# Turning a 512x512 block on VectorE and in the transfers instead of on TensorE, and one stage of products prepared further ahead

## The chip, the cores and the metric

One core of one Trainium2 chip. The metric is the device time of one execution in microseconds; lower is better. Times inside a trace are microseconds from the start of the span.

## The reference

A token mixer gated by a channel MLP, in fp32, for 2048 tokens of 512 numbers:

```python
xn = layernorm(x)                                   # S = 2048, D = 512
s = attention(xn, wqkv) @ wo                        # 32 heads of 16, causal window of 256
y = layernorm(xn)
g = silu(gelu(y @ w1 + b1) @ w2 + b2)               # w1: 512 x 1792, w2: 1792 x 512
out = x + s * g
```

## The kernel before, in words

The attention runs first (to about 432 us of the trace); its output lies in DRAM as `oT_d`, its row sums as `rden_d`. Then the MLP runs over four chunks of 512 tokens. All large products are made of three fp32r products: an operand is split into a high part (an ACT copy to fp32r) and a low part (a VectorE subtraction), and high x high, high x low and low x high are summed.

The loop `for c in range(2)` (lines 1060 to 1155) does chunks 0 and 1. With `c == 1` each iteration `i` of 15 does, in this order:
- `activate(i)`: ACT makes `gelu` of bank `h(i)` into a `t2` tile (five buffers) and its high part `gh(i)`, VectorE the low part `gl(i)`. `gh` and `gl` have two buffers each.
- `project(i - 1)`: twelve products of `gh`, `gl` with w2 into the banks `acc`.
- `hidden(i + 2)`: twelve products of w1 tile i + 2 with the transposed y into a bank of `ps_st` (two banks).
- pieces of other work: the attention output of this chunk is loaded (`load_o`, two transfers), multiplied and split (`split_o`); and y of chunks 2 and 3 is prepared.

That last work is what the change touches. Four tiles of 128 tokens x 512 are loaded (`load_y`, `yp`, four buffers) and normalised twice (`steps2`; statistics on VectorE, a power on GpSimd, the application on ACT): chunk 2 in iterations 0 to 2, chunk 3 in iterations 5 to 7. Then y must be transposed, so that the 512 features lie on partitions as four tiles `kt`. Here `transposed` (line 986) does this by four TensorE transposes per tile into a bank of `ps_yt`: `first_y` for chunk 2 in iterations 3 and 4, `second_y` for chunk 3 in iterations 8 and 10.

Chunks 2 and 3 are then done together: their w1 products are made from seven instead of eight block products, of sums and differences of y and w1 blocks. The inputs are called `11`, `21`, `t1`, `t3`, `t2`, `22` and `t4`; each has two tiles, and each tile a high and a low half in the area of `big` that a w1 tile of chunks 0 and 1 leaves free (`halves_of`): t1 = y3 - y2 of the first half of features, t3 = y3's second half - its first, t2 = y3's second half - t1, t4 = y2's second half - t2. y2 itself is kept meanwhile in `gated[:, 2:4]` and in `kept[1]`. The loop over `g` from line 1160 makes these products.

TensorE, VectorE, ACT and GpSimd issue in the order in which the program is written (`Ordered`, line 32). The queue of transfers, SyncE, does so where `nc.sync.on` is set; elsewhere, so in the whole MLP part, a planner orders it by when it expects each transfer to be ready.

Of the kernel before, what the change touches and what calls it, by code (L numbers as in the profile page):

```python
# [9 lines left out]
F32 = mybir.dt.float32  # L10
# [8 lines left out]
P = 128  # L19
NCH = S // 512  # L20
NKB = S // P
KT = D // P
NF = F // P
# [27 lines left out]
def mixer_kernel(ctx, tc, x, wqk, wv, wo, w1, b1, w2, b2, out):  # L51


    nc = SimpleNamespace(**{name: Ordered(tc, name) for name in ("tensor", "vector", "scalar", "gpsimd", "sync")})

    const = ctx.enter_context(tc.tile_pool(name="const", bufs=1))
    bigp = ctx.enter_context(tc.tile_pool(name="bigp", bufs=1))
    t2 = ctx.enter_context(tc.tile_pool(name="t2", bufs=5))
    small = ctx.enter_context(tc.tile_pool(name="small", bufs=3))
    dram = ctx.enter_context(tc.tile_pool(name="dram", bufs=1, space=bass.MemoryType.DRAM))  # L60
# [8 lines left out]
    def split(dst_hi, dst_lo, src, eng=None):  # L69

        (eng or nc.scalar.copy)(dst_hi, src)
        nc.vector.tensor_sub(dst_lo, src, dst_hi.bitcast(F32))
# [103 lines left out]
    def open_slot(i):  # L176
# [9 lines left out]
    w_d = {"w1": dram.tile([P, NF * 512], F32, name="w1_d"), "w2": dram.tile([P, NF * 512], F32, name="w2_d"),  # L186
           "wo": dram.tile([P, 4 * 512], F32, name="wo_d")}
    g_d = dram.tile([NF, P, 512], F32, name="g_d")
    mT_d = dram.tile([NQ, NCH, 32, P], F32, name="mT_d")


# [6 lines left out]
    ps_st = early.enter_context(tc.tile_pool(name="ps_st", bufs=2, space=PSUM))  # L198
# [24 lines left out]
    ident = const.tile([P, P], F32, name="ident")  # L223
# [360 lines left out]
    mlp = {}  # L584
# [54 lines left out]
    def y_steps(a, b):  # L639
        run(mlp["ln"][a:b])  # L640
# [241 lines left out]
    def load_y(c):  # L882
        if c > 1:
            return load_x(c, ((mlp["yp"], "y"),), "y")
        return [load(mlp["yp"], "y", xn_d[4 * c + i], f"y_{c}_{i}") for i in range(4)]

    def fetch_sums():
        den = t2.tile([P, 512], F32, tag="t2", name="den")
        for g in range(4):
            nc.sync.dma_start(den[32 * g: 32 * g + 32], oT_d[g, :, DH].rearrange("a (c t) -> a c t", c=NCH))  # L890
        return den

    def load_o(c, g):

        cols = slice(512 * c, 512 * (c + 1))
        raw = load(t2, "t2", oT_d[g, :, 0:DH, cols], f"or_{c}_{g}")
        rec = mlp["w2", g // 2][:, 512 * (14 + g % 2): 512 * (15 + g % 2)].bitcast(F32)
        nc.sync.dma_start(rec, bass.AP(tensor=rden_d.tensor, offset=rden_d.offset + 8 * g * S + 512 * c,
                                       ap=[[S, 8], [0, DH], [1, 512]]))
        return raw, rec  # L900
# [70 lines left out]
    def inputs(name, kt, part):  # L971

        return area(halves_of[name, kt])[:, 512 * part: 512 * part + 512]

    yh1 = mlp["yy"][0][0], mlp["yy"][0][1]
    kept = {}
# [6 lines left out]
        first = 256 * (j % (2 if j < 4 else 4))  # L983
        return at[:, first: first + 256 * n]

    def transposed(c, kt):
        ps = ps_yt.tile([P, 512], F32, tag="b", name=f"yt_{c}_{kt}")
        for i in range(4):
            nc.tensor.transpose(ps[:, P * i: P * (i + 1)], mlp["y"][i][:, P * kt: P * (kt + 1)], ident)
        return ps  # L990

    def put(name, kt, src):

        split(inputs(name, kt, 0), inputs(name, kt, 1), src)

    def first_y(kt):

        ps = transposed(2, kt)
        nc.scalar.copy(kept[kt // 2][:, kt % 2], ps)
        put("21" if kt > 1 else "11", kt % 2, ps)  # L1000

    def second_y(kt):

        t1, t4 = kept[0][:, kt], kept[1][:, kt]
        t3, t2_ = (t2.tile([P, 512], F32, tag="t2", name=f"yt{k}_{kt}") for k in (3, 2))
        ps = transposed(3, kt)
        nc.vector.tensor_sub(t1, ps, t1)
        nc.scalar.copy(t3, ps)
        ps = transposed(3, kt + 2)
        nc.vector.tensor_sub(t2_, ps, t1)  # L1010
        nc.vector.tensor_sub(t3, ps, t3)

        def more():
            put("22", kt, ps)
            nc.vector.tensor_sub(t4, t4, t2_)
            put("t1", kt, t1)
            put("t3", kt, t3)

        def most():
            put("t2", kt, t2_)  # L1020
            put("t4", kt, t4)
        return more, most

    raw_w = {}

    def fetch_pair(g):
        raw_w[g] = [load(mlp["yp"], "y", w_d["w1"][:, 512 * f: 512 * f + 512], f"wr_{g}_{f}") for f in (g, g + 7)]
# [32 lines left out]
    for c in range(2):  # L1060
        accs = open_accs(c)
        gs, os_, hs, wanted = {}, [], {}, []
        made = ready if c == 0 else {}

        def hidden(f):
            hs[f] = ps_st.tile([P, 512], F32, tag="b", name=f"h_{c}_{f}")
            for k in range(3 * KT):
                hidden_mm(hs[f], f, k)

        def activate(f):  # L1070
            if f in made and f in soon:
                gs[f] = made[f]
                return
            src = made[f] if f in made else hs.pop(f)
            g = src if f in made and f < 2 else t2.tile([P, 512], F32, tag="t2", name=f"g_{c}_{f}")
            nc.scalar.activation(g, src, AF.Gelu_apprx_tanh, bias=b1s[:, f: f + 1])
            gs[f] = split_g(c, f, g, nc.scalar.copy)

        order = [2, 3, 0, 1, 4, 5, *range(6, NF)] if c == 0 else [*range(NF)]
        if c:  # L1080
            hidden(0)
            hidden(1)
        o_from, o_late = (0, 0) if c else (8, 1)
        for i in range(NF + 1):
            if i < NF:
                activate(order[i])
            if c and i in (1, 2, 6, 7):
                y_steps(6, 10)
            if c and i in (9, 11):
                rest[0]()  # L1090
            if c and i in (9, 12):
                rest[1]()
            if c and i == 14:
                kept["w"] = bigp.tile([P, 768], F32R, tag="wb1", name="wsh")
                combine_w(0)
            if c == 0:
                for kind, f in late_w[LATE[i]: LATE[i + 1]]:
                    settle(kind, f, nc.scalar.copy, nc.vector)
            if i >= 1:
                project(accs, [(order[i - 1], gs.pop(order[i - 1]))], order[0], order[-1])  # L1100
            if i + 2 < NF and order[i + 2] not in made and order[i + 2] > 1:
                hidden(order[i + 2])
            if c == 0:
                if i == 2:
                    den = fetch_sums()
                if 4 <= i < 8:
                    nc.vector.reciprocal(den[:, P * (i - 4): P * (i - 3)], den[:, P * (i - 4): P * (i - 3)])
                    if i == 7:
                        nc.sync.dma_start(rden_d.rearrange("g a (c t) -> (g a c) t", c=NCH), den)
                if i == 4:  # L1110
                    mlp["y"] = load_y(1)
                if i == 6:
                    mlp["ln"] = layernorm(mlp["y"], "C1", False)
                for back, (a, b) in enumerate(((0, 2), (2, 4), (4, 5), (5, 6), (6, 8), (8, 10))):
                    if i == 6 + min(back, 5):
                        y_steps(a, b)
            else:
                steps2(i)
                if i == 3:
                    kept[0] = gated[:, 2:4]  # L1120
                    first_y(0)
                    first_y(1)
                if i == 4:
                    kept[1] = bigp.tile([P, 2, 512], F32, tag="wb1", name="y2_21")
                    first_y(2)
                    first_y(3)
                    mlp["y"] = load_y(3)
                if i in (8, 10):
                    rest = second_y(i // 10)
                if i == 12:  # L1130
                    fetch_pair(0)
            k = i - o_from
            if 0 <= k - 2 - o_late < 4:
                os_.append(split_o(c, k - 2 - o_late, wanted[k - 2 - o_late][0]))
            if 0 <= k - 1 - o_late < 4:
                nc.vector.tensor_mul(wanted[k - 1 - o_late][0], *wanted[k - 1 - o_late])
            if 0 <= k < 4:
                wanted.append(load_o(c, k))
            if c and i in (0, 1, 5, 6):
                y_steps(5, 6)  # L1140
        if c == 0:
            gated = bigp.tile([P, 4, 512], F32, tag="wa", name="gated")

        def between(i):
            if c == 0 and i in (0, 2):
                y_transpose(1, i)
                y_transpose(1, i + 1)
                if i == 2:
                    mlp["y"] = load_y(2)
            if c == 1 and i in (1, 2):  # L1150
                split_w(0, 2 * i - 2)
                split_w(0, 2 * i - 1)
        end_chunk(c, accs, os_, between)
        if c == 0:
            steps2(-1)
# [148 lines left out]
```

## Time and profile before

| | us |
|---|---|
| median of 3 runs | 750.93 (750.61 to 751.13) |
| the profiled execution | 750.88 |
| its span | 749.2 |
| loop `c == 1`, first `hidden` to the last `project` | 489.16 to 568.97 |

In the profile all recorded instructions of the kernel stand at line 43, the helper that issues them, so groups are told apart by engine and tile name: `h` are the banks of `hidden`, `acc` those of `project`, `yt` those of the transposes of y, `s` those of the output product, `xnT` is `big`, `or` and `w` are the two loads of `load_o`, `wr` the raw w1 tiles, `xo` the loads of x for the end of a chunk. A timeline row gives start, duration, engine, operation and operands and, in brackets, how long the engine was idle before it and what ended that. SPq is SyncE's queue: its durations are those of the issue, not of the transfer.

### The profile page before, as it was taken

The page shows a single profiled execution, that of the slowest core. Times are in us where ns is not written, and L with a number is a line of the kernel's source. Part 1 is how long each engine was busy: PE and PEld are TensorE (multiplying, and loading weights), DVE is VectorE, ACT ScalarE, POOL GpSimd, SP SyncE. Part 2 cuts the span into 40 slices and gives each one's busy share as a digit, 9 for nine tenths or more (in the row PEclk, how much of TensorE's full clock was granted, in tenths as well). Part 3 has the DMA queues.
Part 4 walks back from the last instruction along what each step waited for, and adds up shares of the span by engine and source line. Part 5 has one row for each costly group of instructions (what it writes and reads, how often), then busy time and mean ns, then how long its engine had stood idle before and what let it go on. Part 6 is the DMA issues. An engine that isn't in the chain of part 4 may idle for free.

```text
span 749.2 us, 18758 instructions
## 1 busy us (share of the span) xinstructions
PE 733.9 (98%) x7408; PEld 590.4 (79%) x7408; DVE 511.7 (68%) x781; ACT 441.1 (59%) x746; POOL 299.3 (40%) x644
## 2 busy tenths in 40 slices
PE   8999999999999999999999999999999999999997
PEld 7886777777778888777776788888888888888886
DVE  7886777877766778887872648763576765676743
ACT  7757767867667676778877745444463744442001
POOL 7413757767666555767877600120102000001102
PEclk9999999999999999999999999999999999999999
DMA  8633356766555535647724482542012232253611
GB/s 288 191 74 78 84 133 149 201 168 183 152 142 145 144 90 142 162 111 190 200 86 148 133 286 94 165 151 82 31 45 102 93 100 72 70 174 123 222 45 56
DMA packets 56951, 99.40 MB, mean 133 GB/s; under 512 B 11104, under 2 KB 11360, under 8 KB 56864
## 3 DMA queue, kind: packets, MB, share of 16 engines
q1 hardware_dynamic: 56864, 98.21, 45.7%
q8 instruction: 58, 0.95, 0.5%
q14 instruction: 29, 0.24, 0.1%
HBM read 51.39 MB, written 29.62 MB: 108 GB/s over the span
## 4 chain that ended last, share of the span: by engine, by line
PE 89%; ACT 5%; DVE 2%; POOL 2%; issue 1%; DMA 1%; SPq 0%; DVEq 0%; ACTq 0%; POOLq 0%
PE acc L43 20%; PE fb L43 18%; PE zo L43 11%; PE stb L43 9%; PE p L43 9%; PE s L43 6%; PE h L43 6%; PE xy L43 5%; ACT pt L43 4%; PE pv L43 3%; POOL pt L43 1%; DVE xy L43 1%; PE yt L43 1%; DMA x<-in_x_dram 1%; DVE mt L43 0%
## 5 line engine op out<-in xcount | busy, mean ns | idle before, releaser
L43 POOL TENSOR_SCALAR_AFFINE_SELECT pt<-pt 128x256 f32<-128x256 f32 x480 | 193.8, 428 | 132.9 <-ACT pt L43 131.7
L43 ACT ACTIVATE pt<-stb 128x768 f32<-128x768 f32 (+1 forms) x244 | 188.8, 774 | 62.4 <-PE stb L43 54.8
L43 DVE TENSOR_REDUCE mt<-xy 128x4 f32<-128x1024 f32 (+1 forms) x128 | 152.6, 1192 | 4.4
L43 DVE COPY_PREDICATED xy<-upper,zo 128x512 f32<-128x512 int32 x112 | 77.8, 695 | 70.6 <-PE xy L43 63.1
L43 POOL TENSOR_TENSOR xo<-xo,gated 128x512 f32<-128x512 f32 x15 | 20.3, 1358 | 216.8 <-DVE gated L43 192.9
L43 PE MATMUL fb<-xnT,wqb 64*128 64x512 f32 (+1 forms) x684 | 104.8, 397 | 0.3
L43 PE MATMUL zo<-pt,vt 128*17 128x128 f32 x2880 | 103.7, 275 | 0.3 <-POOL pt L43 0.3
L43 PE MATMUL stb<-qk 64*128 64x384 f32 (+1 forms) x488 | 97.2, 393 | 6.2 <-ACT pt L43 4.1
L43 PE MATMUL acc<-w,gh 128*128 128x512 f32 x320 | 98.9, 390 | 0.0
L43 PEld LDWEIGHTS stb<-qk 64*128 64x128 f32 x488 | 45.8, 183 | 51.6 <-ACT pt L43 46.6
L43 PEld LDWEIGHTS zo<-pt,vt 128*17 128x17 f32 x2880 | 67.5, 97 | 15.6 <-issue 6.3
L43 PEld LDWEIGHTS fb<-xnT,wqb 64*128 64x128 f32 (+1 forms) x684 | 64.7, 185 | 11.0 <-DVE pjr L43 1.4
L43 PEld LDWEIGHTS acc<-w,gh 128*128 128x128 f32 x320 | 59.8, 188 | 12.3
L43 PE MATMUL acc<-w,gl 128*128 128x512 f32 x160 | 62.4, 390 | 0.0
L43 PE MATMUL xy<-qk 64*128 64x256 f32 (+2 forms) x536 | 58.4, 291 | 0.2 <-DVE mt L43 0.2
L43 PEld LDWEIGHTS xy<-qk 64*128 64x128 f32 x536 | 46.7, 185 | 6.7 <-issue 3.1
L43 ACT COPY oraw<-zo 128x128 f32<-128x128 f32 x128 | 34.2, 267 | 29.2 <-PE zo L43 28.9
L43 ACT ACTIVATE gated<-acc 128x512 f32<-128x512 f32 x16 | 8.7, 596 | 65.6 <-DVE acc L43 65.6
L43 PE MATMUL s<-wos,ohl 128*128 128x512 f32 (+1 forms) x204 | 44.7, 378 | 0.0
L43 PEld LDWEIGHTS s<-wos,ohl 128*128 128x128 f32 x204 | 36.7, 188 | 7.2 <-DVE gated L43 0.2
L43 PEld LDWEIGHTS zo<-qk 64*128 64x128 f32 x448 | 38.5, 185 | 4.4 <-issue 1.4
L43 ACT COPY p<-p 128x512 f32<-128x512 f32 x21 | 12.3, 586 | 49.7 <-PE p L43 42.3
(195 smaller groups left out, 1241.5 us busy)
## 6 DMA issues: line engine op xcount, KB each, us to landing
qk<-sh SPq DMA_DIRECT2D x128, 128.0 KB
qk<-pjr SPq DMA_DIRECT2D x64, 128.0 KB
oT_d<-oraw SPq DMA_DIRECT2D x32, 256.0 KB
w_d<-in_w_dram SPq DMA_DIRECT2D x14, 512.0 KB
x<-in_x_dram SPq DMA_DIRECT2D x16, 256.0 KB
or<-oT_d SPq DMA_DIRECT2D x16, 256.0 KB
w<-rden_d SPq DMA_DIRECT2D x16, 256.0 KB
xo<-in_x_dram SPq DMA_DIRECT2D x16, 256.0 KB
```

The source lines that it names most:

```text
L43: r = issue(*args, **kwargs)
```

## The change

The transposes of y of chunks 2 and 3 leave TensorE. VectorE's `transpose` turns each 32x32 block of a y tile in place (`turn_y`, two tiles in each of iterations 2, 3, 7 and 8); the tile is written to `z_d` in DRAM; and `fetch_y` reads it back so that the blocks stand where the whole transpose wants them: per feature tile four transfers, each of 32 partitions x 16 blocks x 32 numbers (pieces of 128 B). Chunk 2's tiles are fetched in iteration 3, into `gated[:, 2:4]` and `kept[1]`, and split in iterations 8 and 9; chunk 3's in iteration 8, into low halves of input areas, and combined in iterations 10 to 13. In the loop with `c == 1` SyncE keeps program order. `hidden` runs three tiles ahead there instead of two, and uses the two banks of `ps_yt` beside those of `ps_st`. `transposed`, `first_y`, and the old `second_y` go.

```diff
+    z_d = dram.tile([2, 4, P, 512], F32, name="z_d")
...
+    def turn_y(c, tiles):
+        for i in tiles:
+            y = mlp["y"][i]
+            nc.vector.transpose(y, y)
+            nc.sync.dma_start(z_d[c - 2, i], y)
+
+    def fetch_y(c, kt, dst):
+        for k in range(4):
+            at = z_d[c - 2, 0, 0, 128 * kt + 32 * k: 128 * kt + 32 * k + 32]
+            nc.sync.dma_start(dst[32 * k: 32 * k + 32].rearrange("p (t j) -> p t j", j=32),
+                              bass.AP(tensor=at.tensor, offset=at.offset, ap=[[512, 32], [32 * 512, 16], [1, 32]]))
...
-    def transposed(c, kt):
-        ps = ps_yt.tile([P, 512], F32, tag="b", name=f"yt_{c}_{kt}")
-        for i in range(4):
-            nc.tensor.transpose(ps[:, P * i: P * (i + 1)], mlp["y"][i][:, P * kt: P * (kt + 1)], ident)
-        return ps
...
-    def first_y(kt):
-        ps = transposed(2, kt)
-        nc.scalar.copy(kept[kt // 2][:, kt % 2], ps)
-        put("21" if kt > 1 else "11", kt % 2, ps)
...
+    def fetch_second():
+        for kt, name in ((0, ("t3", 0)), (1, ("t4", 0)), (2, ("22", 0)), (3, ("22", 1))):
+            kept["y3", kt] = inputs(*name, 1).bitcast(F32)
+            fetch_y(3, kt, kept["y3", kt])
...
+    def second_y(i):
+        one, two = ([kept["y3", k + 2 * h] for k in range(2)] for h in range(2))
+        t1, t4 = ([kept[h][:, k] for k in range(2)] for h in range(2))
+        if i == 0:
+            for k in range(2):
+                nc.vector.tensor_sub(t1[k], one[k], t1[k])
+                nc.vector.tensor_sub(scratch("t3", k), two[k], one[k])
+        if i == 1:
+            for k in range(2):
+                put("t1", k, t1[k])
+                put("t3", k, kept["t3", k])
+            for k in range(2):
+                nc.vector.tensor_sub(scratch("t2", k), two[k], t1[k])
+        if i == 2:
+            for k in range(2):
+                put("22", k)
+                put("t2", k, kept["t2", k])
+            for k in range(2):
+                nc.vector.tensor_sub(t4[k], t4[k], kept["t2", k])
+        if i == 3:
+            for k in range(2):
+                put("t4", k, t4[k])
...
-            hs[f] = ps_st.tile([P, 512], F32, tag="b", name=f"h_{c}_{f}")
+            hs[f] = (ps_yt if c and f % 2 else ps_st).tile([P, 512], F32, tag="b", name=f"h_{c}_{f}")
...
-        if c:
-            hidden(0)
-            hidden(1)
+        ahead = 2 + c
+        for f in range(ahead if c else 0):
+            hidden(f)
         o_from, o_late = (0, 0) if c else (8, 1)
+        nc.sync.on = c > 0
...
-            if c and i in (9, 11):
-                rest[0]()
-            if c and i in (9, 12):
-                rest[1]()
+            if c and i >= 10 and i < 14:
+                second_y(i - 10)
...
-            if i + 2 < NF and order[i + 2] not in made and order[i + 2] > 1:
-                hidden(order[i + 2])
+            if i + ahead < NF and order[i + ahead] not in made and order[i + ahead] > 1:
+                hidden(order[i + ahead])
...
+            if c:
+                if i in (2, 3, 7, 8):
+                    turn_y(2 + i // 5, (0, 1) if i in (2, 7) else (2, 3))
+                if i == 3:
+                    mlp["y"] = load_y(3)
+                    kept[0] = gated[:, 2:4]
+                    kept[1] = bigp.tile([P, 2, 512], F32, tag="wb1", name="y2_21")
+                    for kt in range(KT):
+                        fetch_y(2, kt, kept[kt // 2][:, kt % 2])
+                if i in (8, 9):
+                    for kt in (2 * i - 16, 2 * i - 15):
+                        put("21" if kt > 1 else "11", kt % 2, kept[kt // 2][:, kt % 2])
+                if i == 8:
+                    fetch_second()
+                if i == 12:
+                    fetch_pair(0)
             if c and i in (0, 1, 5, 6):
                 y_steps(5, 6)
+        nc.sync.on = False
```

More of the change, by code (lines that the diff above doesn't have):

```diff
@@ L984, in weights @@
         return at[:, first: first + 256 * n]
-    def transposed(c, kt):
-        ps = ps_yt.tile([P, 512], F32, tag="b", name=f"yt_{c}_{kt}")
-        for i in range(4):
-            nc.tensor.transpose(ps[:, P * i: P * (i + 1)], mlp["y"][i][:, P * kt: P * (kt + 1)], ident)
-        return ps
-    def put(name, kt, src):
-        split(inputs(name, kt, 0), inputs(name, kt, 1), src)
-    def first_y(kt):
-        ps = transposed(2, kt)
-        nc.scalar.copy(kept[kt // 2][:, kt % 2], ps)
-        put("21" if kt > 1 else "11", kt % 2, ps)
@@ L1002, in second_y, with high @@
[L1002 to L1022, printed above, removed]
+    def high(name, kt, src=None):
+        at = inputs(name, kt, 1).bitcast(F32) if src is None else src
+        nc.scalar.copy(inputs(name, kt, 0), at)
@@ new lines, in low, with put @@
+    def low(name, kt, src=None):
+        at = inputs(name, kt, 1).bitcast(F32) if src is None else src
+        nc.vector.tensor_sub(inputs(name, kt, 1), at, inputs(name, kt, 0).bitcast(F32))
+    def put(name, kt, src=None):
+        high(name, kt, src)
+        low(name, kt, src)
+    def fetch_second():
+        for kt, name in ((0, ("t3", 0)), (1, ("t4", 0)), (2, ("22", 0)), (3, ("22", 1))):
+            kept["y3", kt] = inputs(*name, 1).bitcast(F32)
+            fetch_y(3, kt, kept["y3", kt])
@@ new lines, in scratch @@
+    def scratch(name, kt):
+        kept[name, kt] = t2.tile([P, 512], F32, tag="t2", name=f"y{name}_{kt}")
+        return kept[name, kt]
+    def second_y(i):
[20 more added lines that the diff above has]
+                put("t4", k, t4[k])
@@ L1118, in mixer_kernel @@
                 steps2(i)
[L1119 to L1131, printed above, removed]
             k = i - o_from
```

## The prediction

> **What bounds the kernel now.** I read the page's busy shares first, then the chain of work that ended last in order of time, then the timelines of the second chunk's loop on each engine, and last the queue of transfers.
>
> ```profile
> PE 733.9 (98%) x7408; PEld 590.4 (79%) x7408; DVE 511.7 (68%) x781; ACT 441.1 (59%) x746; POOL 299.3 (40%) x644
> 497.32 2.72 PE acc L43 x12
> 510.92 2.72 PE h L43 x12
> 513.65 0.87 PE yt L43 x8
> 514.52 2.74 PE acc L43 x12
> 519.98 0.87 PE yt L43 x8
> 539.91 2.79 PE h L43 x12
> 542.71 0.87 PE yt L43 x8
> 554.48 0.88 PE yt L43 x8
> 558.09 2.72 PE h L43 x12
> 560.81 8.16 PE acc L43 x36
> 568.97 10.88 PE s L43 x48
> 489.16:568.97 79.81, 79.81 (x370) 66.30 (x369) 46.86 (x95) 40.72 (x65) 5.75 (x5) 1.00 0.23 74
> ```
>
> The first row is the page, the next ten are the chain, the last is the table by stretch (length, then PE, PEld, DVE, ACT, POOL, clock, DMA share, GB/s) over the loop `c == 1`. PE is busy for all of its 79.81 us at full clock, and the chain runs from one PE piece to the next without a gap. So here a microsecond of matmul taken out is a microsecond of the span, and a microsecond in which PE waits is one more. DVE has 46.86 us of work, ACT 40.72: both have room on the average, so only the order of their work can hurt.
>
> **What is removed.** Four blocks of eight transposes (`yt`): 0.87 + 0.87 + 0.87 + 0.88 = 3.49 us. The block of products behind one takes 2.74 instead of 2.72, and one `h` piece takes 2.79 instead of 2.72; with them 3.6 us. Counted the other way: the new order on PE is four `hidden` pieces, then project(0), and then strictly one `hidden` and one project, so project(i) begins at 489.16 + 4 x 2.72 + 5.44 i = 500.04 + 5.44 i up to i = 10 (554.44), and 11, 12 and 13 follow one another at 557.16, 559.88 and 562.60. The loop ends at 565.32 where it ended at 568.97: 3.65 us. ACT also loses six copies, DVE keeps its subtractions; neither is on the chain.
>
> **What is added on VectorE.** Eight turns of a 128x512 tile. The trace has only turns of 32 columns:
>
> ```profile
> L43 DVE STREAM_TRANSPOSE mT<-mh x32: 198/202/211, 36.7 to 399.2; 128x32 f32<-128x32 f32 x32
> L43 DVE TENSOR_SCALAR veC<-mvC 128x4 f32<-128x4 f32 x3 | 0.5, 170 | 0.1
> 546.38 0.68 DVE L43 TENSOR_TENSOR xnT<-yt,xnT 128x512 fp32r<-128x512 f32 x1
> 546.98 0.68 DVE L43 TENSOR_TENSOR y<-y,yt 128x512 f32<-128x512 f32 x1
> 563.40 0.62 ACT L43 CAST gh<-g 128x512 fp32r<-128x512 f32 x1 [1.04 <-PE acc L43]
> 564.05 0.69 DVE L43 TENSOR_TENSOR gl<-g,gh 128x512 fp32r<-128x512 f32 x1 [1.48 <-ACT gh L43]
> ```
>
> 32 columns cost 202 ns where 4 columns of another operation cost 170, so 1.14 ns a column and 170 + 508 x 1.14 = 0.75 us for 512. The other end is 16 times the whole row, 3.2 us. I take 0.75: a tile of 512 columns is one instruction, and the fixed part is paid once.
>
> **What is added on the queue.** Per chunk four writes of a turned tile to `z_d` and sixteen `fetch_y` of 64 KB, each in pieces of 128 B; SyncE now issues in program order in this loop, so whatever waits holds all behind it. The rows nearest to this:
>
> ```profile
> 457.91 0.32 SPq L43 DMA_DIRECT2D rden_d<-den  x1
> 459.88 0.58 SPq L43 DMA_DIRECT2D w<-rden_d  x1
> 401.74 0.52 SPq L43 DMA_DIRECT2D mT_d<-mT  x1
> 404.46 0.53 SPq L43 DMA_DIRECT2D qk<-mT_d  x1
> 52.08 2.46 SPq L43 DMA_DIRECT2D qk<-sh  x4
> 38.15:38.51 0.36, 0.36 (x6) 0.36 (x5) 0.36 (x1) 0.36 (x3) 0.28 (x2) 1.00 0.30 46
> 38.51:38.80 0.29, 0.29 (x5) 0.29 (x4) 0.29 (x1) 0.29 (x1) 0.21 (x2) 1.00 0.00 0
> 540.00:550.00 10.00, 10.00 (x49) 8.34 (x48) 6.90 (x12) 5.87 (x11) 0.00 (x0) 1.00 0.00 0
> ```
>
> A 256 KB write to DRAM and the issue of what reads it back are 1.97 us apart (457.91 to 459.88); for the 16 KB of `mT`, which go in rows of 128 B, it is 2.72 us. Transfers with such three-part patterns are issued 0.62 us apart (four in 2.46). The stretch 38.15 to 38.51 is one `mT` write alone: 16 KB in 128 B pieces at 46 GB/s, with the 16 DMA engines busy 0.30. So the bounds for one `fetch_y` are 0.62 us, the issue, and 64 KB at that same 46 GB/s, 1.44 us. I take 0.62, since 0.30 busy says that the engines had room for three times the rate (64 KB in some 0.43 us), and since the queue is empty where the second fetch falls (0.00 from 540 to 550). Both ends are kept.
>
> **Which wait ends last.** The first fetch (y of chunk 2) is harmless: y is normalised by 506.13, it is written by about 512, its sixteen transfers are out by about 525, or 537 at the slow end, and its first reader stands behind gh(8), about 536.
>
> ```profile
> 503.19 2.94 ACT L43 ACTIVATE y<-y,shiftC,rsC 128x512 f32<-128x512 f32 x4 [1.87 <-DVE shiftC L43]
> 525.42 0.69 DVE L43 BATCH_NORM_STATS2 bnC<-y 128x6 f32<-128x512 f32 x1
> 530.34 2.94 ACT L43 ACTIVATE y<-y,shiftC,rsC 128x512 f32<-128x512 f32 x4 [5.34 <-DVE shiftC L43]
> 535.90 0.16 DVE L43 SCALAR_TENSOR_TENSOR shiftC<-mvC,rsC 128x4 f32<-128x4 f32 x1 [1.21 <-POOL rsC L43]
> 536.10 2.94 ACT L43 ACTIVATE y<-y,shiftC,rsC 128x512 f32<-128x512 f32 x4 [1.59 <-DVE shiftC L43]
> ```
>
> The second is the one that matters. There are two buffers for `gh`, so gh(i) waits for the end of project(i - 2), as the ACT row at 563.40 shows for the last one (1.04 us idle until PE). gh(5) can start at 519.08, the end of project(3); with 0.62 for gh and 0.60 for gl the statistics of chunk 3's y begin at 520.3 (`load_y(3)`, issued behind the writes at about 514, is there by 517), the first normalisation 4.9 us later (525.42 to 530.34), at 525.2, and the second 5.8 us after that (530.34 to 536.10), with 2.94 to run: done at about 534. Of the four turns, two stand behind gl(7) and two behind gl(8). gl(8) waits for gh(8), which waits for project(6), which ends at 535.40: 0.62 for gh, 0.60 for gl, two turns of 0.75, and the last write is issued at 538.1. The first fetch follows 1.97 us later, 540.1; the sixteenth is issued at 540.1 + 15 x 0.62 = 549.4 and, with 2.72 us from issue to use, there at **552.1**.
>
> What waits for it: `second_y(0)` in iteration 10, whose fourth subtraction needs the last tile; all VectorE work queues behind it, gl(11), gl(12) and gl(13) too, and PE waits for these. From that subtraction to gl(13) there are 1 + gl(11) + 6 + gl(12) + 6 = 15 instructions at 0.60 (546.38 to 546.98) and gl(13) itself at 0.69: 9.7 us. PE needs gl(13) at the third product of project(13), 562.60 + 2 x 0.227 = 563.05. So the fetch may be there as late as 553.3; it has **1.2 us to spare**, 0.08 us per transfer. A second limit does not depend on the fetch: gh(12) cannot start before project(10) ends at 557.16, so gl(12) starts at 557.8, six more at 0.60, and gl(13) ends at 562.7, 0.35 us before PE wants it. If the cover is gone, each microsecond of delay is one of the span. Where it holds, nothing stalls: 750.88 (the profiled execution) - 3.6 = **747.3 us**, against a median of 750.93.
>
> The rest lies beside PE work. `hidden` three ahead in four banks takes the pressure from `gelu`: a bank is needed again only four tiles later, which also removes the 0.07 us above. The loads of `or` and `w` of this chunk now follow the last store of the chunk before (issued by 491.6), eight at 0.62 us, the first needed at 501.40; nothing waits for them:
>
> ```profile
> 488.62 3.02 SPq L43 DMA_DIRECT2D out_dram<-xo  x2
> 501.40 0.68 DVE L43 TENSOR_TENSOR or<-or,w 128x512 f32<-128x512 f32 x1
> ```
>
> **Rivals.**
>
> *The small pieces set the pace (slower).* If a fetch goes at the 46 GB/s of the one row with such pieces, the sixteenth is there at 540.1 + 15 x 1.44 + 2.72 = 564.4, VectorE stands still before gl(11), and PE waits 564.4 - 553.3 = 11.1 us: 758.4 us. It decides from the point where delay eats the gain: 1.2 + 3.6 = 4.8 us over 15 steps, 0.94 us per transfer. Against it speaks the 0.30 busy share; for it, that no row shows more than 16 KB of such pieces at a time, and that SyncE has never issued one with 512 of them. The Trainium skill's DMA: Bandwidth & Descriptors, Specifications, asks for 512 B or more per transfer for line rate, and its VectorE: DVE Perf Modes, The three transpose paths, warns that a plain copy which transposes by strides is "19× slower" than the hardware's own path where the innermost stride at the destination is large, and sends a 128x128 transpose to TensorE. By the first the sum would go to the slow end, 758.4 instead of 747.3; of the second no run here shows the factor, and this change's runs are contiguous at the destination.
>
> *A late tail (still faster).* The fetch is 1 to 3 us later than worked out (0.7 to 0.84 us per transfer, or a longer way to DRAM and back). Then PE waits up to 2 us in front of project(11) to project(13): 747.9 to 749.4 us.
>
> *Turning costs by the block.* At 3.2 us a turn the last write is 2 x 2.45 = 4.9 us later, the fetch there at 557.0, PE waits 3.7 us: 751.0, no change.
>
> *The queue's order holds something up.* With program order, a transfer of the next chunk that the planner lifts in between can wait for VectorE with `load_y(3)` behind it. The second normalisation of chunk 3 has some 2 us to spare before gl(8), so a block of up to 2 us costs nothing, one of 10 us brings the slow rival's times.
>
> **Numbers.** A measurement of this kernel tells about 0.2%, 1.5 us, from no change. Chances: no stall, 0.53 (own range 746.8 to 748.0); late tail 0.13; turning by the block or another delay that just eats the gain, 0.07; slow pieces or a blocked queue 0.27, spread from 752.4 to 758.4. So faster 0.66, same 0.07, slower 0.27. The range runs from 746.8 to 754.5: it takes in the first three cases and a third of the last, and leaves the rest of it out.
>
> **What will show it.** No `yt` on PE, and the `c == 1` loop at 76.2 us without PE idle; STREAM_TRANSPOSE of 128x512 at about 0.75 us; sixteen `fetch_y` 0.62 us apart from about 540 on; `second_y(0)`'s fourth subtraction at about 552, gl(13) ending before 563. Wrong it is if VectorE shows a long idle stretch ended by a transfer into `xnT` and PE one ended by `gl`, or if SyncE's issues of `fetch_y` last a microsecond or more.

## The result, and the profile after

| | before | after |
|---|---|---|
| median, side by side on one chip | 750.75 (750.61 to 751.13) | 747.35 (746.86 to 747.93) |
| the profiled execution | 750.88 | 747.81 |
| its span | 749.2 | 746.1 |
| loop `c == 1` | 489.16 to 568.97: 79.81 | 489.74 to 565.90: 76.16 |

The ratio is 0.9955, 95% interval 0.9941 to 0.997: 3.4 us faster, five runs of each.

The page after: TensorE's busy time fell by 3.0 us with 32 instructions fewer, VectorE's rose by 3.9 with 8 more, and 17,024 packets of less than 512 B were added (11,104 before).

```profile
PE 730.9 (98%) x7376; PEld 587.8 (79%) x7376; DVE 515.6 (69%) x789; ACT 436.9 (59%) x740; POOL 297.8 (40%) x644
DMA packets 75001, 103.61 MB, mean 139 GB/s; under 512 B 28128, under 2 KB 28384, under 8 KB 74912
```

The chain of work that ended last, over the loop (start, length, what), and below it the table by stretch over the same loop:

```profile
489.74 10.88 PE h L43 x48
500.62 2.72 PE acc L43 x12
503.34 2.72 PE h L43 x12
...
552.30 2.72 PE h L43 x12
555.02 10.88 PE acc L43 x48
565.90 10.88 PE s L43 x48
489.74:565.90 76.16, 76.16 (x338) 63.08 (x337) 50.34 (x102) 37.49 (x59) 5.75 (x5) 1.00 0.53 145
```

The `yt` pieces are gone. Four `hidden`, then one project and one `hidden` in turn, then four project: 28 pieces of 2.72 us, without a gap and at full clock. VectorE is 3.5 us busier here, ACT 3.2 less. The loop is 3.65 us shorter; it began 0.58 us later than in the trace of before. Nothing ahead of it was changed, and in nine profiled kernels that share that code (this one and eight of the experiments) it began anywhere from 488.58 to 489.74. So the loop's own length is the sharp measure, and the span has about a microsecond of scatter on it.

VectorE's group of turns, its timeline, SyncE's queue and the table by stretch around the second fetch:

```profile
L43 DVE STREAM_TRANSPOSE y<-y 128x512 f32<-128x512 f32 x8 | 5.3, 693 | 0.3 <-ACT y L43 0.3
537.11 1.30 DVE L43 STREAM_TRANSPOSE y<-y 128x512 f32<-128x512 f32 x2
548.58 0.69 DVE L43 TENSOR_TENSOR yt<-xnT 128x512 f32<-128x512 f32 x1
551.03 0.69 DVE L43 TENSOR_TENSOR yt<-xnT 128x512 f32<-128x512 f32 x1 [1.16 <-DMA xnT<-z_d]
562.48 0.68 DVE L43 TENSOR_TENSOR gl<-g,gh 128x512 fp32r<-128x512 f32 x1
533.34 5.42 SPq L43 DMA_DIRECT2D z_d<-y  x4
540.61 8.42 SPq L43 DMA_DIRECT2D xnT<-z_d  x16
545.00:550.00 5.00, 5.00 (x24) 4.14 (x23) 2.50 (x4) 1.21 (x2) 0.00 (x0) 1.00 0.77 122
```

A turn takes 0.69 us (two in 1.30). The last ends at 538.41, the first fetch is issued 2.2 us later, and sixteen are issued in 8.42 us, 0.53 apart, with the DMA engines 0.77 busy. The fourth subtraction of `second_y(0)` starts at 551.03, after VectorE has waited 1.16 us for the fetch. The last `gl`, gl(13), ends at 563.16. TensorE wants it at the third product of project(13), 555.02 + 3 x 2.72 + 2 x 0.227 = 563.63. So VectorE waited, and TensorE didn't.

### The profile page after: what moved, and what is told of

It is laid out like the page before. It is cut to its first block, busy times and chain, and to the rows that moved or that the text cites. A ratio compares the mean times of both kernels' runs of the same rounds, so it can differ in the third digit from the quotient of the medians.

```text
span 746.1 us, 18779 instructions
## 1 busy us (share of the span) xinstructions
PE 730.9 (98%) x7376; PEld 587.8 (79%) x7376; DVE 515.6 (69%) x789; ACT 436.9 (59%) x740; POOL 297.8 (40%) x644
## 2 busy tenths in 40 slices
DMA packets 75001, 103.61 MB, mean 139 GB/s; under 512 B 28128, under 2 KB 28384, under 8 KB 74912
## 4 chain that ended last, share of the span: by engine, by line
PE 89%; ACT 5%; DVE 2%; POOL 2%; issue 1%; DMA 1%; SPq 0%; DVEq 0%; ACTq 0%; POOLq 0%
PE acc L43 20%; PE fb L43 19%; PE zo L43 11%; PE stb L43 9%; PE p L43 9%; PE s L43 6%; PE h L43 6%; PE xy L43 5%; ACT pt L43 4%; PE pv L43 3%; POOL pt L43 1%; DVE xy L43 1%; DMA x<-in_x_dram 1%; DVE mt L43 0%; ACT pjr L43 0%
## 5 line engine op out<-in xcount | busy, mean ns | idle before, releaser
L43 PEld LDWEIGHTS fb<-xnT,wqb 64*128 64x128 f32 (+1 forms) x684 | 64.6, 185 | 10.9 <-DVE pjr L43 1.4
```

The source lines that it names most:

```text
L43: r = issue(*args, **kwargs)
```

## The experiments

Each was timed beside before, in four to eleven executions. Ratios are to before.

**late_1: the fetch a project later.** The theory says that the fetch has a fixed deadline, and that what passes it is lost in full.

```diff
-                if i in (2, 3, 7, 8):
+                if i in (2, 3, 7, 9):
...
-                if i == 8:
+                if i == 9:
                     fetch_second()
```

> The last two turns of chunk 3 and its fetch are put one iteration later (9 instead of 8). Theory (TensorE is the bound, and the fetch has a deadline): in the changed kernel the turns end at 538.41 and the fourth subtraction starts at 551.03, 12.6 us later. Behind gl(9) the turns end at about 543.9, so the subtraction starts at about 556.5; from it to gl(13) lie 9.7 us, and TensorE wants gl(13) at 563.05 + 0.58 (this trace starts its loop 0.58 us later) = 563.6. So the deadline is 553.9, TensorE waits 2.6 us, and the time is 747.35 + 2.6 = 750.0 us. Rival (VectorE's order has slack that this count misses, or the fetch is off the path altogether): 747.4 us.

Measured: 750.88 us (749.7 to 751.17), ratio 0.9998 [0.9989, 1.0007]; the whole gain is gone. SyncE's queue, VectorE, TensorE, the last piece of the chain in the loop, and the loop's stretch:

```profile
545.72 9.15 SPq L43 DMA_DIRECT2D xnT<-z_d  x16
556.66 0.69 DVE L43 TENSOR_TENSOR yt<-xnT 128x512 f32<-128x512 f32 x1 [0.17 <-DMA xnT<-z_d]
565.70 0.68 DVE L43 TENSOR_TENSOR gl<-g,gh 128x512 fp32r<-128x512 f32 x1
562.22 0.50 PE L43 MATMUL acc<-w,gl 128*128 128x512 f32 x1 [1.18 <-DVE gl L43]
566.44 0.50 PE L43 MATMUL acc<-w,gl 128*128 128x512 f32 x1 [1.20 <-DVE gl L43]
566.44 2.56 PE acc L43 x10
489.42:569.00 79.58, 77.07 (x337) 62.85 (x337) 50.21 (x102) 37.96 (x59) 5.75 (x5) 1.00 0.52 141
```

From the fourth subtraction to the end of gl(13) pass 566.38 - 556.66 = 9.72 us, as the prediction had counted (9.7). The loop starts 0.26 us later than in the trace of before, so the deadline is 553.56; the subtraction is 3.10 us past it, and the loop is 79.58 - 76.16 = 3.42 us longer. So the deadline is real, and where it should be. The 0.3 us beyond the lateness lie behind the last wait: TensorE starts 0.06 us after the end of gl(13), and the ten products from there to the end of the loop take 2.56 us instead of 10 x 0.227 = 2.27; the first is recorded with 0.50 us, where the same product in after has 0.39.

**two_ahead: the third tile ahead taken away.**

```diff
-            hs[f] = (ps_yt if c and f % 2 else ps_st).tile([P, 512], F32, tag="b", name=f"h_{c}_{f}")
+            hs[f] = ps_st.tile([P, 512], F32, tag="b", name=f"h_{c}_{f}")
...
-        ahead = 2 + c
+        ahead = 2
```

> Hidden products two tiles ahead in the two old banks; the turns and transfers stay as changed. Theory: all of the gain is the 32 transposes, the lead is worth at most the 0.07 us piece of the trace before, so 747.4 us. Rival (without the lead a bank waits for gelu while ACT applies the normalisations, 2.9 us each): TensorE stands 1 to 3 us at the hidden products of iterations 5 to 8, 748.4 to 750.4 us.

Measured: 746.84 us (746.76 to 747.04), ratio 0.9946 [0.9934, 0.9959]. Its chain enters and leaves the loop so:

```profile
488.86 8.16 PE h L43 x36
...
565.02 10.88 PE s L43 x48
```

76.16 us, the same to the hundredth. The lead of three tiles and the two further banks are worth nothing in this loop. The median is half a microsecond under that of after; the loop is no shorter, so it isn't from there, and the intervals of the two ratios overlap.

**plain: no turning, and the fetch in whole rows.** It leaves the transposition of y for chunks 2 and 3 out, and shows what the added work costs.

```diff
-            nc.vector.transpose(y, y)
...
+        nc.sync.dma_start(dst, z_d[c - 2, kt])
```

> The turns are left out and every tile is read back as it was written, one transfer of 256 KB in rows of 2 KB instead of four of 64 KB in pieces of 128 B; so y enters the products not transposed. This takes away all that the change adds on VectorE and in small pieces. Theory (what is added lies wholly beside TensorE's work): 747.4 us, as the changed kernel. Rival (the pieces or the eight turns cost something that the trace hides, in the fetches or through gl): 0.5 to 1.5 us faster, 745.9 to 746.9 us.

Measured: 747.35 us (746.97 to 747.6), ratio 0.9953 [0.994, 0.9965]; loop 489.10 to 565.26, again 76.16. With eight turns and 32 transfers in small pieces, or with 8 transfers in whole rows: no difference. The turns and the small pieces are wholly hidden; the writes and the way through DRAM are in both kernels, and TensorE waits for neither.

**queue_free: no program order on SyncE.**

```diff
-        nc.sync.on = c > 0
```

> SyncE's program order is taken away again in the second loop; the rest stays as changed. Theory (only the fetch's deadline counts, and the planner's order keeps the fetch before 553.9): 747.4 us. Rival (the planner puts a load that waits ahead of the writes or the fetches, as it did in the run that also turned chunk 1, where two writes went out 7 us after their turns): TensorE waits 1 to 10 us, 748 to 757 us.

Measured: 747.23 us (746.64 to 747.67), ratio 0.9952 [0.9939, 0.9964]; loop 76.16. SyncE's queue:

```profile
538.71 0.91 SPq L43 DMA_DIRECT2D wr<-w_d  x2
540.50 10.17 SPq L43 DMA_DIRECT2D xnT<-z_d  x16
```

The planner lifts two w1 loads ahead of the fetch and starts it at the same time. Program order isn't what makes the change work. But here the sixteen fetches took 10.17 us to issue instead of 8.42, and the fourth subtraction started at 552.32, 62.71 us into the loop, where after has 61.29: the margin to the deadline is 1.4 us in this trace and 2.9 in that of after.

**pieces_64 and pieces_32.** They were to cut each 128 B piece in two and four.

```diff
+  ... rearrange("p (t s j) -> p t s j", s=2, j=16) ... ap=[[512, 32], [32 * 512, 16], [16, 2], [1, 16]]
```

> The same fetches, each piece cut in two: 1024 pieces of 64 B per transfer instead of 512 of 128 B. In the changed kernel the 16 transfers of chunk 3 are issued 0.53 us apart with the DMA engines 0.76 busy from 540 to 550: 7.6 us for 512 pieces on each of 16 engines, 14.8 ns a piece. Theory (a piece costs its 14.8 ns whatever its size, and there is a deadline at 553.9): 0.95 us per transfer, the last tile 6.3 us later than 551.0, TensorE waits 3.4 us, 750.8 us. Rival (a piece costs by its bytes): 0.47 us per transfer, the issue at 0.53 stays the pace, 747.4 us.

> Pieces of 32 B, 2048 per transfer. Theory (by the piece): 1.9 us per transfer, the last tile 20.5 us later, at 571.5, TensorE waits 17.6 us, 765 us. Rival (by bytes): 747.4 us. This is the slow rival of the prediction brought about on purpose: if it comes, the prediction's mechanism for it was right and only the price of a 128 B piece kept it away.

Measured: 747.01 us (746.75 to 747.78) and 747.2 us (746.88 to 747.32), ratios 0.995 [0.9937, 0.9962] and 0.9952 [0.9938, 0.9965]. Both show the packets of after, 28,128 of less than 512 B: pieces without a gap between them were joined again, on the chip or before it; which of the two, these runs don't show. They tell nothing of small pieces, and count as two repeats of after.

**small_64 and small_32: pieces that are really smaller.** The addresses leave gaps, so the same bytes are moved in 64 B and in 32 B; the fetched y holds other numbers than the transpose.

```diff
-  ... rearrange("p (t j) -> p t j", j=32) ... ap=[[512, 32], [32 * 512, 16], [1, 32]]
+  ... rearrange("p (t j) -> p t j", j=16) ... ap=[[512, 32], [7680, 32], [1, 16]]     # small_64
+  ... rearrange("p (t j) -> p t j", j=8)  ... ap=[[512, 32], [3840, 64], [1, 8]]      # small_32
```

> The two runs with pieces cut in two and four came out as the same transfers as before (28128 packets under 512 B in each): a cut without a gap was joined again. Here each transfer fetches the same 64 KB as 1024 pieces of 64 B with a gap behind each, so the numbers that it fetches are not those of the transpose. Theory (14.8 ns per piece whatever its size, and the deadline at 553.9): 0.95 us per transfer, the last tile 6.3 us later than 551.0, TensorE waits 3.4 us, 747.3 + 3.4 = 750.7 us. Rival (by bytes): 0.47 us per transfer, hidden behind the issue, 747.3 us.

> 2048 pieces of 32 B per transfer, again not those of the transpose. Theory (by the piece): 1.9 us per transfer; the first fetch takes from 518 to 548, the second cannot begin its 30 us before, so the last tile comes at about 582 and TensorE waits some 28 us, 775 us. Rival (by bytes): 747.3 us. In between (a piece of 32 B costs about 10 ns): 1.3 us per transfer, the last tile at about 563, 756 us.

Measured: `small_64` 747.34 us (747.0 to 748.23), ratio 0.9957 [0.9945, 0.997]; `small_32` 760.48 us (759.45 to 760.72), ratio 1.0127 [1.0113, 1.014]. First the hardware queue's row (packets, MB, share of 16 engines) while the second fetch ran: after, 542 to 549; `small_64`, 541 to 549; `small_32`, 545 to 560.

```profile
q1 hardware_dynamic: 6994, 0.94, 81.8%
q1 hardware_dynamic: 12486, 0.81, 106.4%
q1 hardware_dynamic: 23261, 0.74, 86.6%
```

Recorded engine time by packets, over all packets of the window: 16 x 7 us x 0.818 / 6994 = 13.1 ns each, then 10.9, then 8.9. Halving the piece saves less than a fifth of its time. With 32, 64 and 128 pieces to each engine, a 64 KB fetch takes 0.42, 0.70 and 1.14 us by this estimate; the issues were 0.53, 0.66 and 1.27 us apart. A share above 100% means that the recorded times of packets overlap, so the middle one is somewhat too high. Then the end of the fetch, the fourth subtraction and what PE waited for, in `small_64` (three rows; the first is from the chain, from the last issue to its landing) and in `small_32` (the rest, with its queue and one stretch):

```profile
549.36 4.43 DMA xnT<-z_d
553.98 0.69 DVE L43 TENSOR_TENSOR yt<-xnT 128x512 f32<-128x512 f32 x1 [3.38 <-DMA xnT<-z_d]
563.76 0.50 PE L43 MATMUL acc<-w,gl 128*128 128x512 f32 x1 [1.22 <-DVE gl L43]
```

```profile
543.12 20.30 SPq L43 DMA_DIRECT2D xnT<-z_d  x16
566.06 0.69 DVE L43 TENSOR_TENSOR yt<-xnT 128x512 f32<-128x512 f32 x1 [3.53 <-DMA xnT<-z_d]
567.41 0.79 PE L43 MATMUL acc<-w,gl 128*128 128x512 f32 x1 [9.81 <-DVE gl L43]
560.00:565.00 5.00, 0.00 (x0) 0.00 (x0) 1.29 (x2) 1.22 (x2) 0.00 (x0) 0.50 0.89 51
```

`small_64` starts its loop at 488.58: deadline 552.72, subtraction 1.26 us past it, and its loop is 77.75 us long, 1.59 lost. `small_32` starts at 489.15: deadline 553.29, 12.77 us past it, loop 489.15 to 578.42, 13.11 lost. With `late_1` (3.10 past, 3.42 lost) that is one line through three points: what is lost is the lateness and 0.33 us, the 0.3 us of the restart seen in `late_1`. `small_32` is the slow rival, seen: fetches 1.27 us apart, VectorE standing in front of gl(11), TensorE behind it, and slower than before. Some 3 us of the 12.77 come from the first fetch, which held SyncE until 538.0: the second began 53.97 us into the loop (543.12), in after 50.87. The 1.6 us that the profiled `small_64` lost don't show in its median (747.34); its five runs go from 747.0 to 748.23, the profiled one being the slowest. After's own five are as far apart (746.86 to 747.93), so whether the other runs of `small_64` passed the deadline isn't shown.

**Chunk 1's y too.** One transposition of y was left on TensorE in this part, that of chunk 1 during the output product after the first loop: two blocks of eight transposes, 0.87 us each. Three kernels turn it in the same way and differ in how SyncE is ordered; a fourth changes one thing more.

```diff
+                if i in (10, 11):
+                    turn_y(1, (0, 1) if i == 10 else (2, 3))
+                if i == 11:
+                    for kt in range(KT):
+                        fetch_y(1, kt, mlp["yy"][1][kt].bitcast(F32))
+                    mlp["y"] = load_y(2)
...
         def between(i):
-            if c == 0 and i in (0, 2):
-                y_transpose(1, i)
-                y_transpose(1, i + 1)
-                if i == 2:
-                    mlp["y"] = load_y(2)
+            if c == 0 and i > 1:
+                for kt in (2 * i - 4, 2 * i - 3):
+                    hi, lo = mlp["yy"][0][kt], mlp["yy"][1][kt]
+                    nc.scalar.copy(hi, lo.bitcast(F32))
+                    nc.vector.tensor_sub(lo, lo.bitcast(F32), hi.bitcast(F32))
```

*chunk1_too* leaves SyncE to the planner.

> The same for chunk 1: its four tiles are turned in iterations 10 and 11 of the first loop, written, fetched into the low halves of y, and split behind the second and third output product; the 16 transposes before the last output products go, and the load of chunk 2's x moves ahead of them. Theory: two blocks of eight at 0.87 us leave TensorE, 745.6 us. The fetch would be there at about 484 by the pace of the changed kernel (16 in 8.4 us, some 2 us each for the way out and back), and the first hidden products want it at about 488. Rival (the queue orders this part by its plan, and its loads for the output, or a slower fetch beside them, hold the tiles up): TensorE waits before the first hidden product, 746 to 750 us.

Measured: 748.47 us (747.47 to 749.42), ratio 0.9968 [0.9957, 0.9979]. SyncE's queue, and TensorE at the second chunk's first products:

```profile
476.11 0.33 SPq L43 DMA_DIRECT2D y<-in_x_dram  x1
476.53 0.86 SPq L43 DMA_DIRECT2D z_d<-y  x2
480.59 8.81 SPq L43 DMA_DIRECT2D xnT<-z_d  x16
489.24 0.47 PE L43 MATMUL h<-yh,xnT 128*128 128x512 f32 x1 [1.28 <-DVE gated L43]
```

The turns end at 469.5, but the planner had put a load of the next y, which waits for its buffer, ahead of the last two writes: they go out at 476.53, the fetch at 480.59. TensorE stands still for 1.28 us before the second chunk's first product and twice for 0.23 soon after; the row names `gated`, but the chain of waits runs there through the fetch and the splitting of what it brings. The last products of the first loop also take longer, 31.28 us (445.80 to 477.08) instead of 30.18 in after; `chunk1_queue` below has the same delay.

*chunk1_ordered* sets program order from iteration 10 of the first loop to the end of its output product (`nc.sync.on = i >= 10`).

> Chunk 1's y is turned on VectorE too, as in the run before, and from iteration 10 of the first loop on SyncE keeps program order, so that nothing stands between the last turns (469.5 in that run) and their writes. Theory: the fetch begins at about 472 instead of 480.6 and is there at about 482, before the second output product has ended; the 16 transposes are gone at no price, 747.35 - 1.75 = 745.6 us. Rival (VectorE and ACT, not the queue, hold the splits up, or the later loads for the output delay the gating): the first hidden product still waits, 747 to 748.5 us.

Measured: 762.43 us (761.3 to 763.52), ratio 1.0154 [1.014, 1.0168]. SyncE's queue, the longest wait of the output product `s`, and the chain behind that wait:

```profile
473.54 8.29 SPq L43 DMA_DIRECT2D xnT<-z_d  x16
483.88 0.60 SPq L43 DMA_DIRECT2D or<-oT_d  x1
PE s L43 <- DVE ohl L43: 13.9, 1, 13.9
492.61 10.46 PE s L43 x39
```

The last load of the attention output, issued from 464.6 on in after, now stands behind the fetch, which waits for the turns. TensorE waits 13.9 us for what is made of it. The 39 products behind the wait then take 10.46 us, where at the pace of 48 in 10.88 they would take 8.84: the granted clock was 0.50 from 485 to 492.6, the end of the wait, and 0.73 on the average from there to 498.

*chunk1_queue* sets program order for the writes, the fetch and the load of the next y alone, after `load_o` of the iteration.

> Chunk 1's y is turned on VectorE too; program order on SyncE holds only for its four writes, its fetch and the load of chunk 2's x, and they stand behind the last loads of the attention output of chunk 0, which in the run before stood behind the fetch and held the first output product for 14 us. Theory: the fetch begins at about 472 and is there at about 482, the first hidden product waits for nothing, 747.3 - 1.75 = 745.6 us. Rival (the loads of x for the output, now behind the fetch, come late and hold GpSimd's sums and with them the two-tile buffers): 746.5 to 749 us.

Measured: 747.29 us (746.81 to 747.47), ratio 0.9954 [0.9941, 0.9968]: after's time, not 1.75 us less. Chain and VectorE's timeline; the first four rows are after's at the same place.

```profile
446.90 30.18 PE acc L43 x132
477.08 0.87 PE yt L43 x8
467.25 0.69 DVE L43 TENSOR_TENSOR or<-or,w 128x512 f32<-128x512 f32 x1 [1.73 <-DMA w<-rden_d]
471.04 0.68 DVE L43 TENSOR_TENSOR gl<-g,gh 128x512 fp32r<-128x512 f32 x1
```

```profile
472.71 5.30 PE acc L43 x22
478.02 10.88 PE s L43 x48
465.81 0.69 DVE L43 TENSOR_TENSOR or<-or,w 128x512 f32<-128x512 f32 x1 [0.77 <-DMA w<-rden_d]
466.42 1.30 DVE L43 STREAM_TRANSPOSE y<-y 128x512 f32<-128x512 f32 x2
470.79 1.30 DVE L43 STREAM_TRANSPOSE y<-y 128x512 f32<-128x512 f32 x2
472.01 0.65 DVE L43 TENSOR_TENSOR gl<-g,gh 128x512 fp32r<-128x512 f32 x1
```

The second chunk now starts without a wait (`s`, 10.88 in one piece, where after has 0.87 of `yt` before each half). But the tail of project in the first loop, 30.18 us in after, takes 478.02 - 446.38 = 31.64 (the chain enters it at 446.38). VectorE works there without a pause from the arrival of `w` on, and the turns stand ahead of the `gl` for which TensorE waits (1.18 us, at 472.71): from the first use of `w` to that `gl` pass 472.01 - 465.81 = 6.20 us, in after 3.79. The difference, 2.41, is what the two groups of turns fill (2 x 1.22, from each group's start to the next instruction). What was taken off TensorE's path (1.75 us) came back as 1.46 us behind VectorE's. The fetch itself began at 477.82, not at 472 as expected, and was still in time.

*chunk1_act* gives the application of chunk 1's normalisation to ScalarE (`layernorm(mlp["y"], "C1", True)`), to make room on VectorE.

> chunk1_queue with one thing more: the normalisation of chunk 1 (scale and shift of y by the row's statistics) is applied by ScalarE and no longer by VectorE. Theory: with chunk 1's y turned too, the stall of about 1.75 us at the second chunk's transposes is gone, but the first loop ended some 1.6 us later, since VectorE, which is on the path there, got four turns more (4 x 0.65 = 2.6 us). Taking some 4 x 0.5 = 2.0 us off VectorE in the same iterations, and giving it to ScalarE, which has gaps of 1.8 us per iteration there, brings back about 1 us: 746.2 us, and the first loop's last product ends near 477.0 instead of 478.0. Rival: ScalarE's work comes in front of its casts of gh, or the loop is late for another reason than VectorE's load: 747.3 us or more, the first loop ending at 478 or later.

Measured: 746.83 us (745.04 to 748.63), ratio 0.9946 [0.9934, 0.9958]. VectorE, and the chain:

```profile
466.46 0.69 DVE L43 TENSOR_TENSOR or<-or,w 128x512 f32<-128x512 f32 x1 [2.64 <-DMA w<-rden_d]
471.74 0.65 DVE L43 TENSOR_TENSOR gl<-g,gh 128x512 fp32r<-128x512 f32 x1
477.77 10.88 PE s L43 x48
```

The same tail takes 477.77 - 446.12 = 31.65 us, as long as in `chunk1_queue` to a hundredth. The time that was forecast for the tail didn't come, but two things cancel here. From the first use of `w` to the `gl` pass 5.28 us instead of 6.20, so VectorE's chain did get 0.92 us shorter. And `w`, from which that chain starts, was there 6.6 us after its issue (459.84), in `chunk1_queue` after 5.7 (issue 460.11): 0.9 us later. This way scatters where the code up to there is the same: in before, after and the eight experiments on the second loop it took 5.8 us (`pieces_32`) to 7.6 (`pieces_64`). In `pieces_64` the same tail is 31.18 us long although nothing is turned in it. So here the arrival of `w` and VectorE's work behind it set the tail; whether the room is worth the forecast 1 us, one trace of each doesn't tell. The median is 0.5 us under `chunk1_queue`'s, with runs 3.6 us apart; that is no gain that these runs can tell. None of the versions is faster than after beyond the intervals.

## Why the prediction was right, point by point

*What is removed.* Forecast 3.65 us from the loop; it went from 79.81 to 76.16, 3.65. The order of TensorE's pieces was the one written down. That the median also came within 0.1 us of the 747.3 is luck: six kernels with a loop of 76.16 us (after, `two_ahead`, `plain`, `queue_free`, `pieces_64`, `pieces_32`) have medians from 746.84 to 747.35.

*The turn.* Forecast 0.75 us, from 32-column turns; 0.69, two in 1.30. The rival of turning by the block, 3.2 us, is out. The turns fitted beside TensorE's work and cost nothing (`plain`); in the first loop, where TensorE waits for VectorE, the same turns came with 1.5 us lost (`chunk1_queue`). The Trainium skill's VectorE: DVE Perf Modes, Rules for kernel authors, sends a 128x128 transpose to TensorE if its result may lie in PSUM. In this case TensorE sets the time of the second loop, and taking the transposes off it gained 3.65 us there.

*The queue.* Forecast 0.62 us per fetch, 0.53 measured; 1.97 us from write to fetch, 2.2 measured. The engines' limit was put at some 0.43 us per fetch from one small transfer's busy share. By the queue's row it is 32 pieces x 13.1 ns = 0.42 us, below the issue's 0.53: SyncE sets the pace in this trace. In `queue_free` the same sixteen took 10.17 us, 0.64 each. The 1.44 us of the slow end had taken one 16 KB write's rate for that of a stream. The Trainium skill's DMA: Bandwidth & Descriptors, Specifications, asks for 512 B or more per transfer for line rate. The traces agree that larger pieces go faster: the stretch 545 to 550 of after, with the fetch in 128 B pieces, has 122 GB/s at 0.77 busy, and the stretch 534.5 to 538.5 of `plain`, with the fetch in rows of 2 KB, 296 GB/s at 0.90; the line rate itself no run here shows. Even so the slow end, 758.4, didn't come, since the slower fetch still was in time.

*Which wait ends last.* Forecast for the fourth subtraction: 552.1, deadline 553.3, 1.2 us to spare. Measured 551.03 in a trace whose loop started 0.58 later, so 550.45, and 2.9 us to spare; most of the difference is the 15 x 0.09 us of the issue. `late_1`, `small_64` and `small_32` confirm the deadline by lateness. How much is to spare is less certain than these two numbers: in `queue_free`, with the same transfers, it was 1.4 us. A term was left out: each time that the deadline was passed the loop lost 0.33 us beyond the lateness, the slow start of TensorE behind the wait. The second limit was forecast 0.35 us early; gl(13) was 0.47 early.

*Hidden three ahead.* The prediction gave it 0.07 us and no pressure from `gelu`; `two_ahead` has the same 76.16 us without it, so it gives nothing at all.

*The order of SyncE.* It was said that all loads of `or` and `w` go out right behind the last store. The queue held the fourth pair until 507.89, behind the first writes of y. TensorE has no idle time in the loop, so that step was wrong and harmless. The rival, a queue that holds something up, was a real one: `chunk1_ordered` is it, at 13.9 us.

*The slow rival.* Mechanism right, size off for 128 B. Break-even was put at 0.94 us per fetch, counted by the issues alone, with 2.72 us from the last issue to use. `small_64` issued them 10.55 / 16 = 0.66 us apart, which by that count is in time; yet its last fetch landed 4.43 us after the issue, and the deadline was passed by 1.26 us. So transfers that lag behind their issues were left out, and 0.94 is too high: a straight line between `small_64` and `small_32` meets the lost gain at some 0.8 us (an estimate). The loop of that trace still kept 2.06 of the 3.65 us. `small_32`, at 1.27 us per fetch, was 1.27% slower than before.

## What to carry to other kernels

An operation off the bottleneck engine is free only while its result arrives before a deadline that can be worked out by hand, by counting back along the in-order queue from what the bottleneck needs; here the count of 16 instructions gave 9.7 us, and 9.72 were measured. Work it out at each place anew: the same turn was free in one loop, and in the loop before its gain was lost. In a queue with program order, ask first what stands behind the entry that waits; order only the few transfers that need it.

## What the runs showed of the hardware that was not expected

- A strided fetch's pieces cost 13.1, 10.9 and 8.9 ns of recorded engine time at 128, 64 and 32 B: cutting them to a quarter makes a transfer 2.7 times as dear (0.42 to 1.14 us), not four times.
- An access written with two or four pieces that are neighbours in DRAM and in the tile left the packet count at 28,128 (`pieces_64`, `pieces_32`): the pieces were joined again.
- Where TensorE stood still for 9.8 us, the granted clock fell to 0.50 (560 to 565 in `small_32`) and stayed there from 565 to 573; VectorE's chain covered it, since the 13.11 us lost are again the lateness and 0.33. Where nothing covered it, in `chunk1_ordered`, the products behind a wait of 13.9 us took 1.6 us longer (10.46 instead of 8.84).
